# Moving the first expert's weight loads behind the last load of v, in a fused attention and mixture-of-experts kernel

## The chip, the cores and the metric

The kernel runs on one core of one Trainium2 chip, in one launch. The metric is the device time of the launch in microseconds (us). The core has TensorE (PE, with its weight loads as PEld), VectorE (DVE), ScalarE (ACT), GpSimd (POOL) and SyncE (SP); each runs its own instructions in the order in which they were written. In this kernel SP does nothing but issue DMA transfers, and a transfer that has to wait for something holds up those behind it on SP.

## The reference

Three stages follow one another. Attention is chunked: chunks of 32 queries see 16 keys to the left, 8 to the right and 8 memory keys. Its output, 3072 tokens of 512 features, goes through a top-2 mixture of 8 experts and then through a product with a maximum over three matrices.

```python
for c in range(nc):                                   # chunks of 32 queries
    scores = scale * np.matmul(q_c, k_full.transpose(0, 1, 3, 2))
    a = np.exp(scores - np.max(scores, axis=-1, keepdims=True))
    out[:, :, c_start:c_end] = np.matmul(a / (np.sum(a, axis=-1, keepdims=True) + 1e-09), v_full)
...
noisy_logits = x @ w_gate + np.log1p(np.exp(x @ w_noise)) * noise
top2 = np.argpartition(-noisy_logits, 2, axis=1)[:, :2]        # two experts per token
h = np.maximum(x[mask] @ w1[e], 0.0)
out[mask] += top2_w[mask, k, None] * (h @ w2[e])
...
h = np.maximum(np.maximum(x @ w1, x @ w2), x @ w3)
return h @ w_out
```

## The kernel before

**Attention** is a software pipeline over 24 tiles of 128 tokens. `step(t)` writes, in this order: the load of k and q for tile t + 6 (for even t), the scores of tile t + 2, the product with v of tile t (`pv`), the maximum and shift of tile t + 2 on DVE (`shift`), its exponential on ACT (`expo`), the copies of k for tile t + 4 on ACT (`windows`), the transposes of P for tile t + 1 (`ptrans`, into `pt` through ACT), the transposes of the output of tile t - 1 (`xtrans`, into `xt` through ACT), the gate of tile t - 2, some steps of the routing (`pump`, mostly small DVE work), the normalisation of tile t (`norm`: x on DVE, then SP stores x in DRAM as `xd`), and last the load of v for tile t + 3 (`load_v`, two transfers on SP into one of three buffers). Scores lie in one bank of PSUM, sc. The last scores are written in step 21, since step t computes those of tile t + 2.

**Weights** of the experts come as 512 KB parts. `wload` has SP load the next part into one of three staging tiles `st`. `wsplit` turns a part into a high and a low half: ACT copies st into the rounded high half (line 216, CAST), then DVE subtracts it from st to get the low half (line 213), and then the next `wload` follows. Matmuls take three passes (high by high, high by low, low by high). Parts 0 to 3 are w1 of expert 0, parts 4 to 7 its w2, parts 8 to 11 w1 of expert 1.

**Around the change.** Before, three loads are issued after step 15 (WL = 15), and from step 19 on one split follows each step (WS = 19), each with the next load behind it: parts 0 to 4 are split when attention ends, and parts 0 to 7 have their load issued. Unit 0, the first 384 tokens of expert 0, starts at once: eight column blocks f of the first product (12 matmuls each: four tiles of w1 by three passes), which alternate between two PSUM banks, sc and pp. Each is followed by a relu on ACT and the low half of h on DVE, and by one of the remaining splits: seven of them, spread over the eight blocks (none after f = 3). Between unit 0's matmuls `tail` puts what is left of attention (`xtrans` of the last two tiles, their gates) and of the routing (the one-hot tables oh and rc on DVE, their matmuls into tabp on PE). xT, the transposed tokens of unit 0, are gathered from xd and turned in the last steps (`unit_turn`: transposes into the bank xp, a CAST on ACT at line 193 and a subtraction on DVE at line 194).

Tokens for the units after the first can be gathered only when the routing of all tiles is done.

Of the kernel before, what the change touches and what calls it, by code (L numbers as in the profile page):

```python
# [23 lines left out]
NT = N // 128  # L24
# [7 lines left out]
PU = [1, 3, 5]  # L32
HOLD = 1
OHN = 4
WL = 15
WS = 19
NV = 3
RG = [6, 4, 3, 5, 3, 3]
G0 = 2
# [11 lines left out]
def tile_kernel(ctx, tc, qT, kT, mkT, vw, wgn, noise, w1, w2, m2w, out):  # L51
    nc = tc.nc
    PE, ACT, DVE, POOL, SP = nc.tensor, nc.scalar, nc.vector, nc.gpsimd, nc.sync
# [41 lines left out]
    def spin(o, n, joined=False):  # L95

        for i in range(n):
            if n == 10:
                mm(o, ones_r[:, 0:128], ones_r[:, 0:512], start=not joined or i == 0, stop=not joined or i == n - 1)
            else:  # L100
                mm(o, ones, warm, start=(i == 0), stop=(i == n - 1))
# [72 lines left out]
    def wtile(i):  # L174
        return slots[i % WB]

    def wload():
        n = wnext[0]
        if n == len(wparts):
            return  # L180
        wnext[0] += 1
        if isinstance(wparts[n], int):
            src = wsrc[wparts[n]] if wparts[n] < W0 else m2f[wparts[n] - W0]
            st = wst[n] = stage.tile([128, 1024], F32, name="st")
            o = st.rearrange("p (i d) -> p i d", i=2) if len(src.shape) == 3 else st
            SP.dma_start(o, src)
        else:
            _, j, h = wparts[n]
            st = wst[n] = stage.tile([128, 1024], I32, name="st")
            SP.dma_start(st, m2i[j, :, 1024 * h:1024 * h + 1024])  # L190
# [4 lines left out]

    formed = []

    def wsplit(eng=None):
        for task in wtasks()[1:]:
            task(eng)  # L200

    def wtasks():

        n = wnext[1]
        if n == len(wparts):
            return [n]
        wnext[1] += 1
        st = wst.pop(n)
        if isinstance(wparts[n], int):
            w = wtile(wparts[n])  # L210

            def low(eng):
                (eng or POOL).tensor_tensor(w[:, 1, :], st, w[:, 0, :].bitcast(F32), op=ALU.subtract)  # L213
                wload()

            return [n, lambda eng: ACT.copy(w[:, 0, :], st), low]  # L216
        _, j, h = wparts[n]
        return [n] + narrow(st.rearrange("p (n t) -> p n t", t=2), j, h)
# [77 lines left out]
    def unit_turn(u, j):  # L296
        if u < len(units) and j < len(fetched[u]):
            g, n = fetched[u][j]
            turn(g, n, xTs[u], 128 * j, None if u else 0)
# [14 lines left out]
    def load(t):  # L314
        b, i = divmod(t, TB)
        if i == 0:
            m_t[b] = ld.tile([128, HP, 8], F32, name="mk", bufs=2)
            SP.dma_start(m_t[b], mkT[b])
        if i % 2 == 0:
            eng = SP if t < 6 else ACT  # L320
            k_t[t] = ld.tile([128, HP, 280], F32, name="k")
            q_t[t] = ld.tile([128, 2, HP, 128], F32, name="q")
            for j in range(2) if t == 0 else [slice(0, 2)]:
                ks = slice(0, 280) if t else slice(152 * j, 152 + 128 * j)
                eng.dma_start(k_t[t][:, :, ks], kT[b, i // 2, :, :, ks])
                eng.dma_start(q_t[t][:, j], qT[b, i // 2, :, j])
            k_t[t + 1], q_t[t + 1] = k_t[t], q_t[t]
# [223 lines left out]
    def pump(n, tensor=True):  # L551

        for r in routes:
            r[1] -= 1
        moved = 1
        while n > 0 and moved:
            moved = 0
            for r in routes[:]:
                if n and r[1] <= 0 and (r[2] not in ("rank", "count", "table") or tensor) and (
                        r[2] != "rank" or r[3] == ranked[0]) and (r[2] != "table" or r is routes[0]):  # L560
                    r[2] = next(r[0], "end")
                    n, moved = n - 1, 1
                    if r[2] == "end":
                        routes.remove(r)
                    elif r[2]:
                        r[1] = hold[0]
# [19 lines left out]
    def turns_of_first():  # L586
        if 0 in fetched:
            turned[0] += 1
            if turned[0] > UH:
                unit_turn(0, turned[1])  # L590
                turned[1] += 1

    def do(f, u, *pr):
        if 0 <= u < NT:
            f(u, *pr)

    def pairs(f, t):
        for pr in range(HP):
            do(f, t, pr)

    def step(t):
        if t + 6 < NT and t % 2 == 0 and t >= 0:
            load(t + 6)
        pairs(scores, t + 2)
        if t <= 0:
            spin(idle, 10 if t < 0 else 6, t == -1)
        pairs(pv, t)
        do(shift, t + 2)
        do(expo, t + 2)
        do(windows, t + 4)  # L610
        pairs(ptrans, t + 1)
        if t < NT - 2:
            pairs(xtrans, t - 1)
            pairs(gate, t - 2)
        turns_of_first()
        pump(PU[1], False)
        do(norm, t)
        if t == NT - 2:
            pairs(gate, t - 2)
            pairs(xtrans, t - 1)  # L620
        if t >= 0:
            do(load_v, t + NV)
        if t < NT - 2:
            pump(PU[2], False)
        else:
            pump(PL)
# [13 lines left out]
    for t in range(-2, NT):  # L640
        step(t)
        if t == WL:
            for _ in range(3):
                wload()
        if t >= WS:
            wsplit(DVE)
        turns_of_first()
    while 0 not in fetched:
        pump(1000)
    while turned[1] < 4:  # L650
        unit_turn(0, turned[1])
        turned[1] += 1
    passing.close()


# [123 lines left out]
    def task_of(part, now, i):  # L779
        if i == 0:  # L780
            now += wtasks()
            assert wparts[now.pop(0)] == part
        now[i](DVE)

    def unit(u):
# [3 lines left out]
        if u == 0:  # L789
            side = spread([partial(wsplit, DVE)] * (len(plan[0]) + 8 - wnext[1]), 8) + [[] for _ in range(8, steps)]  # L790
        else:
            side = [[] for _ in range(steps)]
            for part, *at in plan[u]:
                now = []
                for i, t in enumerate(at):
                    side[t].append(partial(task_of, part, now, i))
# [77 lines left out]
    def second(xT, dst, step=lambda s: None, middle=lambda s: None, along=[]):  # L874

        h = [big.tile([128, 2, 512], F32R, name=f"h{i}") for i in range(6)]
        for f in range(3):
            ms = big.tile([128, 2, 512], F32, name=f"h{6 + f % 2}")
            for w in range(3):
                l = quads.pop(3 * f + w)  # L880
                for r in range(2):
                    step(6 * f + 2 * w + r)
                    p = psum("p")
                    for k in range(4):
                        if k == 2:
                            middle(6 * f + 2 * w + r)
                        three(p, [l[:, (k // 2) ^ (3 * r), k % 2, c, :] for c in range(2)],
                              parts(xT, k, slice(0, 512)), k == 0, k == 3)
                    m = ms[:, r, :]
                    if w == 0:  # L890
                        ACT.copy(m, p)
                    else:
                        DVE.tensor_tensor(m, m, p, op=ALU.max)
                    if w == 2:
                        split(m, h[2 * f + r][:, 0, :], h[2 * f + r][:, 1, :], DVE)
        step(18)
        side = spread(along, 24)
        side[4].insert(0, partial(middle, 19))
# [110 lines left out]
    def block(b):  # L1009
        t0, nt = blocks[b]  # L1010

        def step(s):
            if nt == 8:
                for k, task in ((8, block_turn), (0, block_fetch), (6, block_mix)):
                    if s >= k and (s - k) % 7 == 0:
                        task(b + 1, (s - k) // 7)
                return
            if s % 2 == 0 and s >= 4:
                block_mix(b + 1, s // 2 - 2)
            if b == 0 and s in (1, 3, 5):  # L1020
                quad_load((6, 7, 8)[s // 2])
            if b == 0 and s in (2, 5, 8):
                wsplit(DVE)
            if b == 0 and s == 6:
                ring_load()
            if b == 0 and s == 18:
                for _ in range(3):
                    ring_load()
# [125 lines left out]
```

## Time and profile before

| | |
|---|---|
| median of 3 runs | 1154.63 us (1151.62 to 1158.38) |
| the profiled execution's own time | 1149.49 us |
| its span, first to last instruction | 1147.7 us |
| mean granted TensorE clock | 0.995 of full |
| PE busy | 1106.3 us, 96% of the span |
| DVE, ACT, POOL busy | 55%, 34%, 19% of the span |

The profiled execution was 5.1 us shorter than the median of the runs, and 1.8 us of its time lie outside its span. PE is busy nearly everywhere after the first 165 us, so what a change before that point does to the end is read from when PE gets through the work of that stretch.

### The profile page before, as it was taken

The page shows a single profiled execution, that of the slowest core. Times are in us where ns is not written, and L with a number is a line of the kernel's source. Part 1 is how long each engine was busy: PE and PEld are TensorE (multiplying, and loading weights), DVE is VectorE, ACT ScalarE, POOL GpSimd, SP SyncE. Part 2 cuts the span into 40 slices and gives each one's busy share as a digit, 9 for nine tenths or more (in the row PEclk, how much of TensorE's full clock was granted, in tenths as well). Part 3 has the DMA queues.
Part 4 walks back from the last instruction along what each step waited for, and adds up shares of the span by engine and source line. Part 5 has one row for each costly group of instructions (what it writes and reads, how often), then busy time and mean ns, then how long its engine had stood idle before and what let it go on. Part 6 is the DMA issues. An engine that isn't in the chain of part 4 may idle for free. (4 is left out here: it accounts for less than half of the span.)

```text
span 1147.7 us, 17323 instructions
## 1 busy us (share of the span) xinstructions
PE 1106.3 (96%) x6803; PEld 927.2 (81%) x6804; DVE 632.7 (55%) x1258; ACT 391.6 (34%) x680; POOL 215.9 (19%) x237
## 2 busy tenths in 40 slices
PE   7987899999999999999999999999999999999997
PEld 5876778889888888888888887888877878887886
DVE  4586873373474645755646645334765586655221
ACT  5777432232422423424324233222411252113110
POOL 3001010100001001100110020243365525533000
PEclk9999899999999999999999999999999999999999
DMA  8998551261473554755834765375577635668301
GB/s 246 301 291 275 178 167 56 96 214 61 145 247 101 159 172 128 221 149 173 248 97 156 233 192 198 125 230 178 147 220 219 213 120 160 199 182 276 128 1 40
DMA packets 113689, 199.06 MB, mean 173 GB/s; under 512 B 8576, under 2 KB 46592, under 8 KB 113600
## 3 DMA queue, kind: packets, MB, share of 16 engines
q1 hardware_dynamic: 76736, 109.86, 30.4%
q0 software_dynamic: 34272, 78.13, 22.6%
q10 hardware_dynamic: 2592, 9.88, 2.8%
q8 instruction: 56, 0.92, 0.3%
q14 instruction: 33, 0.27, 0.1%
HBM read 151.18 MB, written 46.66 MB: 172 GB/s over the span
## 5 line engine op out<-in xcount | busy, mean ns | idle before, releaser
L93 PE MATMUL sc<-xT,w 128*128 128x512 f32 (+3 forms) x912 | 193.6, 359 | 5.1 <-DVE h L811 3.8
L93 PE MATMUL pp<-xT,w 128*128 128x512 f32 (+3 forms) x912 | 190.5, 356 | 0.0
L93 PEld LDWEIGHTS sc<-xT,w 128*128 128x128 f32 x912 | 157.3, 188 | 29.1 <-ACT h L807 3.1
L93 PEld LDWEIGHTS pp<-xT,w 128*128 128x128 f32 x912 | 157.4, 188 | 19.5 <-DVE h L811 0.2
L264 POOL DMA_INDIRECT g<-xd,tok x56 | 55.1, 984 | 531.3 <-PE idle L271 242.4
L93 PE MATMUL po<-w,h 128*128 128x512 f32 x548 | 135.0, 395 | 0.0
L93 PE MATMUL misc<-w,h 128*128 128x512 f32 x522 | 127.8, 394 | 0.0
L93 PE MATMUL tabp<-w,h 128*128 128x512 f32 x498 | 121.5, 394 | 0.0
L93 PEld LDWEIGHTS po<-w,h 128*128 128x128 f32 x548 | 101.0, 188 | 20.5
L93 PEld LDWEIGHTS misc<-w,h 128*128 128x128 f32 x522 | 96.5, 188 | 19.8
L93 PEld LDWEIGHTS tabp<-w,h 128*128 128x128 f32 x498 | 92.2, 188 | 18.9
L811 DVE SCALAR_TENSOR_TENSOR h<-sc,h 128x256 fp32r<-128x256 f32 (+2 forms) x96 | 39.9, 443 | 91.0 <-ACT h L807 91.0
L213 DVE TENSOR_TENSOR w<-st,w 128x1024 fp32r<-128x1024 f32 x67 | 81.0, 1217 | 11.2 <-ACT w L216 11.0
L811 DVE SCALAR_TENSOR_TENSOR h<-pp,h 128x256 fp32r<-128x256 f32 (+2 forms) x96 | 39.9, 443 | 71.6 <-ACT h L807 71.6
L216 ACT CAST w<-st 128x1024 fp32r<-128x1024 f32 x67 | 70.1, 1046 | 4.4 <-DMA st<-in_w 4.0
L807 ACT ACTIVATE h<-sc 128x512 fp32r<-128x512 f32 (+3 forms) x64 | 33.1, 517 | 111.4 <-PE sc L93 108.7
L264 POOL DMA_INDIRECT g<-ys,rows x48 | 50.6, 1053 | 101.3 <-DMA ys<-y 61.9
L807 ACT ACTIVATE h<-pp 128x512 fp32r<-128x512 f32 (+3 forms) x64 | 33.1, 517 | 80.3 <-PE pp L93 80.2
L93 PE MATMUL po<-v,pt 128*32 128x130 f32 x768 | 30.1, 294 | 17.7 <-ACT pt L383 8.9
L251 ACT CAST top<-val 128x1024 fp32r<-128x1024 f32 x18 | 18.9, 1049 | 80.2 <-DVE val L246 68.3
L194 DVE TENSOR_TENSOR xT<-xp,xT 128x512 fp32r<-128x512 f32 (+1 forms) x35 | 23.3, 666 | 37.8 <-ACT xT L193 37.8
L93 PEld LDWEIGHTS po<-v,pt 128*32 128x32 f32 x768 | 22.3, 115 | 24.2 <-ACT pt L383 12.6
(197 smaller groups left out, 1564.4 us busy)
## 6 DMA issues: line engine op xcount, KB each, us to landing
st<-in_w SPq DMA_DIRECT2D x64, 512.0 KB
w<-m2s POOLq DMA_DIRECT2D x27, 1024.0 KB
st<-in_m2w SPq DMA_DIRECT2D x24, 512.0 KB
ys<-y SPq DMA_DIRECT2D x48, 256.0 KB
m2s<-top SPq DMA_DIRECT2D x18, 512.0 KB
m2s<-val SPq DMA_DIRECT2D x18, 512.0 KB
xT<-m2s POOLq DMA_DIRECT2D x9, 1024.0 KB
w<-m2s POOLq DMA_DIRECT2D x9, 768.0 KB
```

The lines of the kernel that those rows point to most:

```text
L93: PE.matmul(o, l, r, start=start, stop=stop)
L194: (eng or POOL).tensor_tensor(lo, src, hi.bitcast(F32), op=ALU.subtract)
L213: (eng or POOL).tensor_tensor(w[:, 1, :], st, w[:, 0, :].bitcast(F32), op=ALU.subtract)
L216: return [n, lambda eng: ACT.copy(w[:, 0, :], st), low]
L251: ACT.copy(hi[0], full)
L264: POOL.indirect_dma_start(out=g[0:n], out_offset=None, in_=src, in_offset=bass.IndirectOffsetOnAxis(ap=idx, axis=0))
L807: ACT.activation(h[:, 0, 0:n], p[:, 0:n], AF.Relu)
L811: DVE.scalar_tensor_tensor(o[:, c], p[:, c], 0.0, h[:, 0, c].bitcast(F32), op0=ALU.max, op1=ALU.subtract)
```

## The change

The three first loads are issued after step 20, which is the step with the last load of v (WL = 20). Splits are written inside step 21, 22 and 23, right behind the place of the exponential (WS = 21): one in each of the first two, two in the last, so that four parts instead of five are split when attention ends. Only the first of these four is followed by a load (part 3); the other three loads, parts 4 to 6, are issued together after the last step. Unit 0 now has eight splits in its first product, one behind each block.

```diff
-WL = 15
-WS = 19
+WL = 20
+WS = 21
...
-    def wsplit(eng=None):
-        for task in wtasks()[1:]:
+    def wsplit(eng=None, more=True):
+        for task in wtasks(more)[1:]:
             task(eng)
...
                 (eng or POOL).tensor_tensor(w[:, 1, :], st, w[:, 0, :].bitcast(F32), op=ALU.subtract)
-                wload()
+                if more:
+                    wload()
...
         do(expo, t + 2)
+        if t >= WS:
+            for _ in range(1 + (t == NT - 1)):
+                wsplit(DVE, t == WS)
         do(windows, t + 4)
...
-        if t >= WS:
-            wsplit(DVE)
         turns_of_first()
     while 0 not in fetched:
         pump(1000)
     while turned[1] < 4:
         unit_turn(0, turned[1])
         turned[1] += 1
+    for _ in range(3):
+        wload()
     passing.close()
```

In the rows that follow, the numbers after a tile's name tell its allocations apart; w0 to w8 are the parts, P the shifted scores, L375/L376 their exponential. First SP, from the store of x of tile 20 to the first parts that unit 0 splits. Before:

```order
L401 DMA xd_57<-x_1846 128x512
L334 DMA v2_136<-in_vw 56x1040 x2
L186 DMA st_1858<-in_w2 128x2x512
L401 DMA xd_57<-x_1921 128x512
L186 DMA st_1932<-in_w2 128x2x512
L401 DMA xd_57<-x_1971 128x512
L186 DMA st_1999<-in_w2 128x2x512
L401 DMA xd_57<-x_2032 128x512
L186 DMA st_2052<-in_w2 128x2x512
```

And after the change:

```order
L402 DMA xd_57<-x_1836 128x512
L335 DMA v2_136<-in_vw 56x1040 x2
L186 DMA st_1846<-in_w1 128x1024
L186 DMA st_1848<-in_w1 128x1024
L186 DMA st_1850<-in_w1 128x1024
L186 DMA st_1893<-in_w1 128x1024
L402 DMA xd_57<-x_1917 128x512
L402 DMA xd_57<-x_1965 128x512
L402 DMA xd_57<-x_2026 128x512
L186 DMA st_2044<-in_w2 128x2x512
```

The first expert's w1 now stands behind the last v, and its w2 behind the last store of x (tile 23). Second, ACT from the exponential of tile 22 to the first turn of xT (L193). Before:

```order
L216 CAST w0_122<-st_1460 128x1024
L375 ACTIVATE P_1817<-P_1817 128x512
L383 COPY pt_1824<-pp_93 128x512
L409 COPY xt_1830<-xp_95 128x512
L216 CAST w1_123<-st_1462 128x1024
L375 ACTIVATE P_1896<-P_1896 128x512
L383 COPY pt_1903<-pp_93 128x512
L409 COPY xt_1909<-xp_95 128x512
L216 CAST w2_124<-st_1464 128x1024
L193 CAST xT0_130<-xp_95 128x4x128
```

And after the change:

```order
L376 ACTIVATE P_1807<-P_1807 128x512
L384 COPY pt_1814<-pp_93 128x512
L410 COPY xt_1820<-xp_95 128x512
L376 ACTIVATE P_1888<-P_1888 128x512
L217 CAST w0_122<-st_1846 128x1024
L384 COPY pt_1899<-pp_93 128x512
L410 COPY xt_1905<-xp_95 128x512
L193 CAST xT0_130<-xp_95 128x4x128
L217 CAST w1_123<-st_1848 128x1024
```

The two casts ahead of the exponentials of tiles 22 and 23 are gone, and the first cast stands between the exponential of tile 23 and pt of tile 22. Third, DVE between the last turn of xT (L194) and x of tile 23. Before:

```order
L424 TENSOR_TENSOR csum0_118<-csum1_119,add_1994 128x8
L213 TENSOR_TENSOR w3_125<-st_1780,w3_125 128x1024
L194 TENSOR_TENSOR xT0_130<-xp_95,xT0_130 128x4x128
L424 TENSOR_TENSOR pr_2023<-E1_109,idle_94 128x80
L485 TENSOR_REDUCE rank_115<-pr_2023 128x2x5
L396 TENSOR_SCALAR rs_2029<-po_96 128x8
L397 RECIPROCAL rs_2029<-rs_2029 128x8
L399 TENSOR_TENSOR x_2032<-po_96,rs_2029 128x512
```

And after the change:

```order
L425 TENSOR_TENSOR csum0_118<-csum1_119,add_1988 128x8
L194 TENSOR_TENSOR xT0_130<-xp_95,xT0_130 128x4x128
L213 TENSOR_TENSOR w2_124<-st_1850,w2_124 128x1024
L213 TENSOR_TENSOR w3_125<-st_1893,w3_125 128x1024
L425 TENSOR_TENSOR pr_2017<-E1_109,idle_94 128x80
L486 TENSOR_REDUCE rank_115<-pr_2017 128x2x5
L397 TENSOR_SCALAR rs_2023<-po_96 128x8
L398 RECIPROCAL rs_2023<-rs_2023 128x8
L400 TENSOR_TENSOR x_2026<-po_96,rs_2023 128x512
```

One split ahead of the turn became two behind it, ahead of the routing's pr and rank and of x. In unit 0 every block's split moves by one part: behind f = 0 stands part 4 where part 5 stood, and behind f = 3, where none stood, part 7.

## Rows read from the trace of the kernel before

**Rows 1.** The page: busy tenths of PE in 40 slices of the span.

```profile
PE   7987899999999999999999999999999999999997
```

**Rows 2.** Windows: each engine's busy us (instructions), granted clock, DMA share, GB/s.

```profile
120.00:140.00 20.00, 16.79 (x172) 14.79 (x163) 16.12 (x49) 10.44 (x19) 0.00 (x0) 0.83 0.50 157
140.00:160.00 20.00, 18.58 (x129) 17.25 (x128) 18.16 (x57) 9.72 (x17) 0.00 (x0) 1.00 0.52 161
180.00:200.00 20.00, 20.00 (x99) 18.24 (x98) 6.61 (x19) 4.91 (x9) 0.00 (x0) 1.00 0.01 3
```

**Rows 3.** Timeline of PE: start, us, instructions, idle before and its releaser.

```profile
89.84 1.08 PE L93 MATMUL sc<-kw,q 128*32 128x128 f32 x32
...
104.53 1.08 PE L93 MATMUL sc<-kw,q 128*32 128x128 f32 x32
107.88 1.96 PE L93 MATMUL po<-v,pt 128*32 128x130 f32 x32 [2.27 <-ACT P L375]
...
112.47 1.08 PE L93 MATMUL sc<-kw,q 128*32 128x128 f32 x32
...
117.80 1.08 PE L93 MATMUL sc<-kw,q 128*32 128x128 f32 x32
...
134.02 1.33 PE L93 MATMUL sc<-xT,w 128*128 128x384 f32 x3
```

**Rows 4.** Timeline of SP: when transfers were issued.

```profile
93.09 1.62 SPq L186 DMA_DIRECT2D st<-in_w  x3
...
99.16 1.72 SPq L334 DMA_DIRECT2D v<-in_vw  x2
...
119.26 0.37 SPq L401 DMA_DIRECT2D xd<-x  x1
...
126.55 0.38 SPq L186 DMA_DIRECT2D st<-in_w  x1
```

**Rows 5.** DMA view, 80 to 160 us: issues and KB (1024 bytes) of each.

```profile
st<-in_w SPq DMA_DIRECT2D x13, 512.0 KB
xd<-x SPq DMA_DIRECT2D x11, 256.0 KB
v<-in_vw SPq DMA_DIRECT2D x10, 227.5 KB
```

**Rows 6.** Windows around the loads and the slow clock, columns as in rows 2.

```profile
93.00:107.00 14.00, 10.65 (x211) 9.19 (x209) 10.84 (x33) 10.41 (x15) 0.00 (x0) 1.00 1.03 319
108.00:111.00 3.00, 3.00 (x43) 2.61 (x43) 0.66 (x4) 1.59 (x2) 0.01 (x1) 0.50 0.42 132
120.20:125.10 4.90, 2.78 (x34) 2.35 (x28) 4.61 (x21) 2.37 (x4) 0.00 (x0) 0.99 0.89 252
128.00:130.00 2.00, 1.48 (x12) 1.38 (x10) 0.67 (x2) 1.37 (x3) 0.00 (x0) 0.90 0.69 255
```

**Rows 7.** Timeline of ACT and DVE around steps 19 to 21.

```profile
108.68 0.94 ACT L346 COPY kw<-k 64x896 f32<-64x896 f32 x1
...
114.67 1.23 DVE L213 TENSOR_TENSOR w<-st,w 128x1024 fp32r<-128x1024 f32 x1 [2.94 <-ACT w L216]
...
119.82 1.23 DVE L213 TENSOR_TENSOR w<-st,w 128x1024 fp32r<-128x1024 f32 x1 [0.31 <-ACT w L216]
...
122.73 0.63 ACT L375 ACTIVATE P<-P 128x512 f32<-128x512 f32 x1 [2.94 <-DVE P L372]
123.27 0.57 ACT L383 COPY pt<-pp 128x512 f32<-128x512 f32 x1
```

**Rows 8.** Timeline of DVE, ACT and PE in unit 0.

```profile
134.93 0.69 DVE L399 TENSOR_TENSOR x<-po,rs 128x512 f32<-128x512 f32 x1
...
138.41 1.04 ACT L216 CAST w<-st 128x1024 fp32r<-128x1024 f32 x1
139.35 0.59 ACT L409 COPY xt<-xp 128x512 f32<-128x512 f32 x1
...
140.30 0.37 PE L93 MATMUL tabp<-rc,oh 128*128 128x56 f16 x8
...
141.11 0.51 PE L93 MATMUL misc<-wg_sb,xt 128*128 128x16 f32 x4
...
151.71 0.32 PE L93 MATMUL tabp<-rc,oh 128*128 128x56 f16 x6 [0.67 <-DVE rc L424]
```

More of the change, by code (lines that the diff above doesn't have):

```diff
@@ L196, in tile_kernel, with wtasks @@
     formed = []
-    def wsplit(eng=None):
-        for task in wtasks()[1:]:
+    def wsplit(eng=None, more=True):
+        for task in wtasks(more)[1:]:
             task(eng)
-    def wtasks():
+    def wtasks(more=True):
         n = wnext[1]
```

## The prediction

> **What bounds the kernel now.** I began with the page's line of PE in slices: PE is at nine tenths or more from the eighth slice on and has its gaps in the first six, some 170 us [rows 1]. The windows by 20 us say which stretch is loose: PE is busy 16.8 of 20 us from 120 to 140, at a mean clock of 0.83, 18.6 from 140 to 160, and all of 180 to 200 [rows 2]. So the change can only win or lose where it is made, between the loads at 93 us and some 165 us, and what it does to PE there it does to the end. In that stretch DVE is the second engine to look at: 16.1 and 18.2 of 20 us busy [rows 2].
>
> The timeline of PE shows the end of attention step by step, by the starts of the scores [rows 3]. Steps 16 to 18 took (104.53 - 89.84) / 3 = 4.90 us each, step 19 took 7.94. In it PE stood 2.27 us ahead of the product with v of tile 19, and that product then took 1.96 us where the scores, of the same count, take 1.08. The page names ACT's exponential as what PE waited for, but v of tile 19 is the likelier one: its load was issued at 99.16, behind the three weight loads of 93.09 [rows 4], while the DMA engines were busy without a break (share 1.03 at 319 GB/s from 93 to 107) [rows 6]. Three loads are 3 x 524 = 1573 thousand bytes [rows 5], 4.9 us at that rate. From 108 to 111 the granted clock was 0.50 [rows 6], that is 1.2 instead of 2.4 GHz, after PE had stood; 3 us at half rate cost 1.5 us.
>
> **The change part by part.** I follow one number, the lead: how much earlier than before the same instruction comes.
>
> *Step 19, won.* Without weight loads in front, v of tile 19 lands some 4.9 us earlier, which is more than the 2.27 us it was late. The lead at step 20 lies between 7.94 - 4.90 = 3.0 and 2.27 + 1.5 = 3.8 us. ACT's last copy of k ends at 109.6 [rows 7] and pt of tile 20 comes behind it, so not all of this is free; I take 3.5.
>
> *Steps 20 and 21, won.* DVE's two splits at 114.67 and 119.82 (1.23 us each) stood ahead of the shifts of tiles 22 and 23 [rows 7]. The scores of 22 were done at 112.47 + 1.08 = 113.55 and the first split at 115.9, so the shift came 2.3 us late; the second split ended at 121.05, and DVE had other work up to 119.5, so 1.5 late. Both together are worth between 2.5 (the splits alone) and 3.8; I take 3.2, since the routing's exponentials on ACT then come next. The exponential of tile 23 moves from 122.73 [rows 7] by 6.7 to 116.0 and ends at 116.65. The store of x of tile 20 stands ahead of the second split, so it wins less: 5.2, from 119.26 [rows 4] to 114.1.
>
> *The first cast, lost.* Behind that exponential ACT now meets the cast of part 0, and pt of tile 22 is queued behind it, which PE's product of tile 22 waits for. When does part 0 land? Before, the same three things stood in a row on SP: xd, the two halves of the last v, one weight load; 262 + 466 + 524 = 1252 thousand bytes [rows 5]. From 120.20 to 125.10 the engines moved 4.9 x 252 = 1235 [rows 6], so the load landed at about 125.1, 5.8 us after xd was issued. The load is now issued some 0.5 us sooner behind v: I take 5.3, that is 119.4. The nearest bound below is a load by itself: issued at 126.55 [rows 4], moved from 128 to 130 (510 thousand bytes) [rows 6], 3.45 us, which from 115.4 gives 118.8. The bound above is that the second and third load take a share meanwhile; the next rival prices it. ACT stands from 116.65 to 119.4, casts for 1.04, and pt of tile 22 comes at 120.45 instead of 123.27 [rows 7]: the lead falls to 2.8. PE stands longer than before at this place, so I leave it the stretch at half rate that it had there. Parts 1 to 3 land 1.6 to 2 us after one another and are not waited for. Part 3's load waits on SP for the split of part 0, with the stores of x of tiles 21 to 23 queued behind it; x of tile 21 comes after that split on DVE anyway, so this costs nothing.
>
> The Trainium skill (DMA: Bandwidth & Descriptors, section Queues, rings and completion order) says that each DMA engine consumes the descriptors of a ring in order; by that rule part 0 is not slowed by parts 1 and 2, the landing at 119.4 stands and with it the 0.7 us of the sum, and without it B's 4.2 would be due. No row here shows one of three queued loads landing.
>
> *Unit 0's start.* From there the chain (turns, product of tile 23) is the same; the first matmul moves from 134.02 [rows 3] to 131.2.
>
> *Two splits in a row, lost on DVE.* Behind the last turn DVE now has the low halves of parts 2 and 3, ACT their two casts, where before one split stood ahead of the turn. That is one split more (1.23) and about 1.0 us of waiting for the first cast ahead of pr, rank and x of tile 23: x, at 134.93 [rows 8], has a lead of only 0.6 us and starts at 134.3.
>
> *The cast of part 4, lost on ACT.* Its load stands behind xd of tile 23 on SP, so it is issued at about 135.5 and lands, by the 3.45 us of the lone load, at 138.9. ACT meets the cast behind the relu of f = 0, which comes 2.8 us earlier than before, and so it waits some 3 us. Queued behind it is xt of tile 23, which ends at 140.6 (before: 139.35 + 0.59 = 139.94 [rows 8]). PE needs it for the gate of tile 23, at 141.11 [rows 8]: with xt at 140.6 the lead is 0.5. The tables ahead of it (140.30) don't decide: rc comes 0.6 us earlier by DVE's lead and 1.2 by the split of part 4 that no longer stands in front.
>
> *The split behind f = 3, lost.* DVE gets 1.22 us more just where PE already waits 0.67 us for its rc at 151.71 [rows 8], in a window where DVE is 91% busy [rows 2]. Between 0 (if DVE's idle 1.8 us of that window take it) and 1.22; PE's wait says that there is no slack, and I take 1.2. Ahead of it 0.5 was left, so PE is 0.7 us late, and stays so.
>
> Sum: + 3.5 + 3.2 - 3.9 - 2.3 - 1.2 = -0.7, so 0.7 us longer. The profiled execution's own 1149.5 would be 1150.2; on the median of the runs, 1154.63, that is **1155.3 us**.
>
> **The rivals.** *A: the lead holds.* The parts land as lone loads do, DVE takes the extra splits into its idle time (3.9 and 1.8 us from 120 to 160 [rows 2]), and the gates wait for nothing; the 2.8 us at unit 0's first matmul reach the end: 1151.8. For it: PE, not DVE, is nearly full there. Against it: the rc wait, and that xd of tile 23 must be stored before part 4 is loaded. It decides if part 4 lands before about 136.7.
>
> *B: slower, the three loads land together.* Then ACT waits for 262 + 466 + 3 x 524 = 2300 thousand bytes instead of 1252, at 300 GB/s 3.5 us more, and everything behind pt of tile 22 is that much later: 0.7 + 3.5 = 4.2, 1158.8. It begins to decide when part 0 lands after 120.7, and from 118.7 on there is nothing left to win. For some of it speaks that 252 GB/s from 120.20 to 125.10 is less than the 319 of the fuller stretch [rows 6], so a load can be slow; against it, that the load of before landed about when its own bytes and those ahead of it were through. The rule of the Trainium skill on ring order above speaks against it too. A second stretch at half rate in unit 0, after the waits for rc and xt, would cost 1.5 us and comes on top.
>
> *C: the change doesn't do what it says.* If v of tile 19 is late through k, q and v alone, step 19 stays at 7.94, and the rest gives 0.7 + 3.5 = 4.2 us: 1158.8 as well. The bytes speak against it: without the loads the busy stretch would be 4.9 us shorter.
>
> **How the numbers follow.** My forecast, with its own bounds (part 0 between 118.8 and 120.7, the last split between 0 and 1.2), is 1153.5 to 1156.6: 0.56. A 0.23, B 0.15, C 0.06. A range of 1151.0 to 1158.8 takes in the middle of each, and about 2 in 10 of the chance lie outside. A measurement of this kernel can tell about 0.5% from no change, here 5.8 us. No case gives that much by itself: a faster result needs A with the half clock gone too (0.08), a slower one B or C with a second stretch at half rate (0.07). Within 0.5%: 0.85.
>
> **What would show it.** In the profile after: step 19 at about 4.5 to 5 us and no half clock near 108; the cast of part 0 with a wait of 2 to 3 us for the DMA behind the exponential of tile 23; unit 0's first matmul near 131; x of tile 23 near where it was; a wait of ACT for part 4's load of about 3 us; PE's wait for rc in the fifth routing group grown from 0.67 to nearly 2 us, and the last table matmuls within 1 us of before. I am wrong if the casts don't wait, or if routing ends as much earlier as unit 0 starts.

## The result and the profile after

The changed kernel is slower: 1161.82 us (median of 9 runs) against 1151.8 us (9 runs of before), a ratio of 1.0094 [1.0078, 1.011]. The prediction was 1155.3 us with a range up to 1158.8, so it was wrong. It counted from 1154.63, the median of the first three runs of before; in its own terms it expected 0.7 us more than before, and 10.0 us came.

The profiled execution took 1160.44 us with a span of 1158.6. It is already 1.14 us behind the one of before at the scores of tile 18 (90.98 us against 89.84 in [rows 3]), ahead of everything that the change touches; I take that off below. The timeline of PE, columns as in [rows 3]:

```profile
90.98 1.08 PE L93 MATMUL sc<-kw,q 128*32 128x128 f32 x32
...
100.56 1.08 PE L93 MATMUL sc<-kw,q 128*32 128x128 f32 x32
...
104.28 1.08 PE L93 MATMUL sc<-kw,q 128*32 128x128 f32 x32
106.98 1.09 PE L93 MATMUL po<-v,pt 128*32 128x130 f32 x32 [1.62 <-ACT pt L384]
...
109.98 1.08 PE L93 MATMUL sc<-kw,q 128*32 128x128 f32 x32
...
126.27 1.12 PE L272 MATMUL xp<-ident,g 128*128 128x128 f32 x4 [6.23 <-ACT xt L410]
128.00 1.96 PE L93 MATMUL po<-v,pt 128*32 128x130 f32 x32 [0.62 <-DVE x L400]
...
137.08 1.33 PE L93 MATMUL sc<-xT,w 128*128 128x384 f32 x3
...
147.80 0.62 PE L93 MATMUL misc<-wg_sb,xt 128*128 128x16 f32 x4 [2.75 <-ACT xt L410]
...
150.92 2.27 PE L93 MATMUL sc<-xT,w 128*128 128x384 f32 x6
...
162.43 0.32 PE L93 MATMUL tabp<-rc,oh 128*128 128x56 f16 x6 [1.64 <-DVE rc L425]
...
173.97 0.32 PE L93 MATMUL tabp<-rc,oh 128*128 128x56 f16 x6 [1.10 <-DVE rc L425]
```

Two things are to be seen. The start is won, though not quite where it was forecast: step 19 takes 109.98 - 104.28 = 5.70 us where it took 7.94 (forecast: 4.5 to 5), with PE still waiting 1.62 us for pt. The product with v runs at full speed, and there is no slow stretch near 108 us. Then PE stands twice, 6.23 us ahead of 126.27 and 2.75 us ahead of 147.80, each time for a copy of xt on ACT. In [rows 8] the gate of tile 23 stood at 141.11, without a wait.

The last tables come at 173.97 us. Before, the same group stood 11.5 us behind the 151.71 of [rows 8], as here behind 162.43:

```profile
163.20 0.32 PE L93 MATMUL tabp<-rc,oh 128*128 128x56 f16 x6 [1.10 <-DVE rc L424]
```

What follows is alike: 1158.6 - 173.97 = 984.6 us here, 1147.7 - 163.20 = 984.5 before. So the whole loss lies ahead of the last tables. ACT's timeline shows what xt waited for:

```profile
118.98 0.63 ACT L376 ACTIVATE P<-P 128x512 f32<-128x512 f32 x1 [2.35 <-DVE P L373]
124.20 1.04 ACT L217 CAST w<-st 128x1024 fp32r<-128x1024 f32 x1 [4.59 <-DMA st<-in_w]
125.15 0.58 ACT L384 COPY pt<-pp 128x512 f32<-128x512 f32 x1
125.63 0.59 ACT L410 COPY xt<-xp 128x512 f32<-128x512 f32 x1
...
146.22 1.04 ACT L217 CAST w<-st 128x1024 fp32r<-128x1024 f32 x1 [4.50 <-DMA st<-in_w]
147.17 0.58 ACT L410 COPY xt<-xp 128x512 f32<-128x512 f32 x1
```

Both casts wait for their load some 4.5 us, with pt and xt queued behind them. The timeline of SP says when the loads were issued; a row joins issues that follow each other:

```profile
117.05 0.37 SPq L402 DMA_DIRECT2D xd<-x  x1
...
118.35 8.51 SPq L186 DMA_DIRECT2D st<-in_w  x4
127.97 13.06 SPq L402 DMA_DIRECT2D xd<-x  x3
141.13 7.78 SPq L186 DMA_DIRECT2D st<-in_w  x4
```

Part 0 arrives for ACT 7.15 us after xd was issued (124.20 - 117.05), and part 4 5.1 us after its own issue at 141.13; the prediction gave them 5.3 and 3.45. The windows of the same execution, columns as in [rows 2]:

```profile
120.00:140.00 20.00, 12.09 (x117) 10.26 (x117) 10.92 (x33) 9.13 (x16) 0.00 (x0) 0.66 0.42 142
140.00:160.00 20.00, 16.83 (x100) 15.81 (x99) 13.52 (x41) 7.70 (x15) 0.00 (x0) 0.83 0.51 168
...
121.80:126.20 4.40, 0.00 (x0) 0.00 (x0) 0.92 (x1) 2.00 (x3) 0.00 (x0) 0.50 0.74 294
126.20:131.40 5.20, 4.51 (x43) 3.61 (x44) 4.31 (x19) 1.84 (x4) 0.00 (x0) 0.50 0.49 151
...
149.00:154.00 5.00, 5.00 (x25) 4.39 (x24) 2.81 (x8) 1.52 (x3) 0.00 (x0) 0.50 0.51 147
```

Against [rows 2] PE does 4.7 us less work from 120 to 140 and 1.8 less from 140 to 160. In the first stand and behind each of the two the granted clock is 0.50 (1.2 of 2.4 GHz) for a while. The lead, 1.14 us taken off, as predicted and as measured:

| place | predicted lead, us | measured lead, us |
|---|---|---|
| scores at 112.47 of [rows 3] | 3.5 | 3.6 |
| exponential of tile 23 | 6.7 | 4.9 |
| pt of tile 22 | 2.8 | -0.7 |
| unit 0's first matmul | 2.8 | -1.9 |
| gate of tile 23 | 0.5 | -5.5 |
| tables of the fifth group | -0.7 | -9.6 |

### The profile page after: what moved, and what is told of

Its sections match the earlier page's. It is cut to its first block, busy times and chain, and to the rows that moved or that the text cites. A ratio compares the mean times of both kernels' runs of the same rounds, so it can differ in the third digit from the quotient of the medians.

```text
span 1158.6 us, 17319 instructions
## 1 busy us (share of the span) xinstructions
PE 1109.7 (96%) x6803; PEld 930.6 (80%) x6804; DVE 632.9 (55%) x1258; ACT 392.2 (34%) x680; POOL 216.3 (19%) x237
## 5 line engine op out<-in xcount | busy, mean ns | idle before, releaser
L213 DVE TENSOR_TENSOR w<-st,w 128x1024 fp32r<-128x1024 f32 x67 | 81.0, 1218 | 16.3 <-ACT w L217 16.1
L194 DVE TENSOR_TENSOR xT<-xp,xT 128x512 fp32r<-128x512 f32 (+1 forms) x35 | 23.3, 666 | 39.0 <-ACT xT L193 38.9
L193 ACT CAST h<-h 128x128 fp32r<-128x128 f32 (+1 forms) x60 | 18.2, 363 | 66.8 <-DVE h L897 51.7
```

The costliest lines, as they stand in the source:

```text
L193: ACT.copy(hi, src)
L194: (eng or POOL).tensor_tensor(lo, src, hi.bitcast(F32), op=ALU.subtract)
```

## The experiments

My theory was that the two waits for loads are the whole loss, and that the load arrives later than the bytes moved per us say. The rivals: the loads slow one another (the prediction's B), the new place of the splits costs by itself, or the half rate does. "Before" in the ratios is run on the same chip beside each.

| run | what it is | median, us | ratio to before |
|---|---|---|---|
| the change | both waits | 1161.82 | 1.0094 [1.0078, 1.011] |
| e1_loads_early | first loads behind step 15 | 1158.6 | 1.0061 [1.0041, 1.008] |
| e2_first_alone | part 0 loaded alone | 1161.8 | 1.0088 [1.0064, 1.0113] |
| e3_loads_follow | each split followed by its load | 1154.6 | 1.0030 [1.0012, 1.0048] |
| e4_wl17 | first loads behind step 17 | 1155.98 | 1.0049 [1.0028, 1.007] |
| e6_wl17_follow | both of these | 1151.02 | 0.9995 [0.9978, 1.0012] |
| e7_before_wl17 | before, first loads behind step 17 | 1148.09 | 0.9976 [0.9961, 0.999] |
| e8_split_end | e3, splits at the ends of the steps | 1154.9 | 1.0042 [1.0024, 1.0061] |
| e9_spin | the change, matmuls into the wait | 1158.63 | 1.0072 [1.005, 1.0094] |
| e10_gather | e6, gathers later | 1149.06 | 0.9987 [0.9972, 1.0002] |
| e11_ws20_wl17 | e6, splits from step 20 on | 1150.28 | 0.9998 [0.9981, 1.0016] |
| e12_before_wl17_gate | e7, gathers later | 1146.98 | 0.9971 [0.9954, 0.9989] |

### Loads early, and the first load alone

**e1_loads_early** is the change with `WL = 15` as before; the splits and the last three loads stay in their new places.

```
-WL = 20
+WL = 15
```

> The changed kernel, but its first three loads are issued after step 15, as before the change; splits and the loads of parts 4 to 6 stay where the change put them. Theory 1 (the loss is two waits of ACT for loads, 4.6 us at the cast of part 0 and 4.5 us at that of part 4, with what PE loses behind them): the first wait goes, the stand ahead of the product with v of tile 19 comes back (2.3 us and a stretch at half rate), the second wait stays near 4.5 us; some 5 to 7 us above the kernel before, 3 to 5 below the changed one. Rival (the place of the splits costs: ahead of pt, two in a row ahead of x of tile 23, one more behind f = 3): no better than the changed kernel, 10 us above before.

The first cast waits for nothing (122.24 us). The cast of part 4 still waits 4.20 us and the gate of tile 23 2.50. v is late again: PE waits 2.15 us for it, here in step 17. Steps 17 to 19 together take 18.1 us, as before the change, against 14.5 in the change. So against before, which stands there too, most of the loss is left without the first wait.

**e2_first_alone** loads part 0 alone behind the last v, and the next parts only behind later steps.

```
-                wsplit(DVE, t == WS)
+                wsplit(DVE, False)
...
-        if t == WL:
-            for _ in range(3):
-                wload()
+        for _ in range({20: 1, 21: 2, 22: 1}.get(t, 0)):
+            wload()
```

> The changed kernel, but only part 0 is loaded behind the last v; parts 1 and 2 are issued behind the store of x of tile 21, part 3 behind that of tile 22. If part 0 lands late because the loads of parts 1 and 2 share the DMA engines with it: ACT's wait at the cast of part 0 falls from 4.6 to 2 to 3 us and part 0 lands 5 to 5.5 us after the store of x of tile 20 is issued (7.15 in the changed kernel). If it is late because a load behind the last v takes that long anyway: the wait stays at 4 to 5 us. In total 0 to 3 us below the changed kernel by the first, within 1 us of it or slower by the second.

ACT still waits 4.29 us for part 0 (4.59 in the change), so the parts behind it slow it by 0.3 us at most, and rival B falls. By itself the load shows what the prediction left out. The windows by 1 us, the last column the GB/s (here also the thousand bytes moved in the window):

```profile
118.00:119.00 1.00, 0.80 (x32) 0.56 (x25) 0.91 (x6) 0.17 (x1) 0.00 (x0) 1.00 0.01 4
119.00:120.00 1.00, 1.00 (x31) 0.80 (x23) 0.97 (x4) 0.00 (x0) 0.00 (x0) 1.00 0.61 213
120.00:121.00 1.00, 1.00 (x13) 1.00 (x10) 0.48 (x1) 0.49 (x1) 0.00 (x0) 1.00 0.74 207
121.00:122.00 1.00, 0.57 (x6) 0.47 (x5) 0.00 (x0) 0.14 (x1) 0.00 (x0) 1.00 0.93 241
122.00:123.00 1.00, 0.00 (x0) 0.00 (x0) 0.00 (x0) 0.00 (x0) 0.00 (x0) 1.00 0.96 198
123.00:124.00 1.00, 0.00 (x0) 0.00 (x0) 0.00 (x0) 0.00 (x0) 0.00 (x0) 0.67 0.97 381
124.00:125.00 1.00, 0.00 (x0) 0.00 (x0) 0.00 (x0) 0.00 (x0) 0.00 (x0) 0.50 0.08 29
```

The end of it in windows of 0.2 us, and the cast:

```profile
124.80:125.00 0.20, 0.00 (x0) 0.00 (x0) 0.00 (x0) 0.00 (x0) 0.00 (x0) 0.50 0.05 20
125.00:125.20 0.20, 0.00 (x0) 0.00 (x0) 0.00 (x0) 0.00 (x0) 0.00 (x0) 0.50 0.00 0
```

```profile
125.43 1.04 ACT L217 CAST w<-st 128x1024 fp32r<-128x1024 f32 x1 [4.29 <-DMA st<-in_w]
```

From 118 to 124 us 4 + 213 + 207 + 241 + 198 + 381 = 1244 thousand bytes moved, nearly as many as xd, v and part 0 have (1252). Nothing is queued behind them. Yet the load is not over at 124: a share of 0.05 stays until 125.0, about what one of the core's 16 DMA engines makes (1/16 = 0.06), and then there is nothing. The load is complete only when its slowest engine is through, about 1 us behind the rest. The cast starts at 125.43, 0.4 us after the last bytes and 1.4 us after the point at which the sum of the bytes says that the load is there. The Trainium skill (DMA: Bandwidth & Descriptors, section Anatomy of one DMA — SWDGE (gpsimd) path) says that the semaphore update can't fire until the last byte is confirmed landed; the trace agrees, as the cast starts behind the last engine's bytes. The Trainium skill puts, in the same section, about 2.0 us of fixed cost on a transfer, most of it that confirmation, for GpSimd's path; this load went by SP, and its trace shows 0.4 us. Why one engine is behind the others is not shown.

### One wait at a time

**e3_loads_follow** issues a load behind each split, as before the change, and drops the three loads behind attention. Part 4 is then issued early, part 0 as in the change.

```
-                wsplit(DVE, t == WS)
+                wsplit(DVE)
...
-    for _ in range(3):
-        wload()
```

> The changed kernel, but each split is followed by its load, as before the change, so that parts 4 to 6 are loaded in steps 22 and 23 and not together behind the store of x of tile 23. Theory 1: the wait at the cast of part 4 (4.5 us), PE's wait for xt behind it (2.75 us) and the stretch at half rate near 150 us go, the wait at the cast of part 0 stays; 4 to 6 us below the changed kernel. Rival (place of the splits): within 1 us of the changed kernel.

It came 0.64% below the change, a little more than the 4 to 6 us expected. On ACT the first wait stays (4.23 us), the second is gone:

```profile
122.09 1.04 ACT L217 CAST w<-st 128x1024 fp32r<-128x1024 f32 x1 [4.23 <-DMA st<-in_w]
...
139.19 1.04 ACT L217 CAST w<-st 128x1024 fp32r<-128x1024 f32 x1
```

**e4_wl17** is the change with `WL = 17`, so that the first wait goes and the second stays.

> The changed kernel with nothing but the step of the first loads changed, 17 instead of 20: part 0 is there when its cast comes, while part 4's load still stands behind the last store of x. With it the four cases of the two waits are complete: neither (0.9995), the first alone (1.0030), both (1.0094). If the two waits add up, the second alone stands at 0.9995 + 0.0064 = 1.006, with the cast of part 4 waiting some 4 us and the gate of tile 23 some 2.5. If the first wait only makes the second worse (the half rate behind it, the late store), the second alone costs less, 1.002 to 1.004.

```profile
120.97 1.03 ACT L217 CAST w<-st 128x1024 fp32r<-128x1024 f32 x1
...
142.04 1.04 ACT L217 CAST w<-st 128x1024 fp32r<-128x1024 f32 x1 [5.61 <-DMA st<-in_w]
```

The gate of tile 23 waits 2.60 us, and the matmuls behind it run at half rate, 1.31 us for three. The 1.0049 lies between the two expectations.

**e6_wl17_follow** has both edits: `WL = 17`, and each split followed by its load.

> Both waits taken away at once: the changed places of the splits, but the first three loads are issued after step 17 (behind the v of tile 20, so that the v of tile 19 is ahead of them) and each split is followed by its load. Theory 1: no cast waits for a load, PE does not stand at tile 19; 0 to 4 us below the kernel before. Rival (place of the splits): 4 us or more above the kernel before.

No cast waits, and the loss is gone. The four cases fit together: over e6 the first wait costs 0.35%, the second 0.54%, both 0.99%. A plain sum would be 0.89%, and each ratio is known to about 0.2%, so whether the two make each other worse can't be told. It is shown, though, that with neither nothing of the loss is left that this measurement could tell (0.2%).

### What stands behind the waiting cast, and the clock

**e8_split_end** is e3 with the splits at the ends of the steps, so that pt of tile 22 and xt of tile 20 stand ahead of the first cast on ACT.

```
-        if t >= WS:
-            for _ in range(1 + (t == NT - 1)):
-                wsplit(DVE)
         do(windows, t + 4)
...
+        if t >= WS:
+            for _ in range(1 + (t == NT - 1)):
+                wsplit(DVE)
         turns_of_first()
```

> The loads as in the run with each split followed by its load (first load behind step 20), but the splits at the ends of steps 21 to 23, so that ACT meets the first cast behind pt of tile 22 and xt of tile 20 and no longer ahead of them. That run stood at 1.0030 [1.0012, 1.0048]. If its loss comes from pt of tile 22 queued behind the waiting cast, this run comes back to the kernel before: 0.999 to 1.001, and pt of tile 22 comes some 4 us earlier than there. If the loss comes from the late part itself (the casts and splits behind it late, whatever waits in front), it stays near 1.003.

pt goes ahead, and the time does not come back: 1.0042, no better than e3's 1.0030. ACT's timeline, and then PE's:

```profile
120.66 0.56 ACT L384 COPY pt<-pp 128x512 f32<-128x512 f32 x1
...
126.22 1.04 ACT L217 CAST w<-st 128x1024 fp32r<-128x1024 f32 x1 [4.51 <-DMA st<-in_w]
```

```profile
129.18 1.11 PE L272 MATMUL xp<-ident,g 128*128 128x128 f32 x4 [5.15 <-DVE xT L194]
```

The same lateness now goes through DVE: the split waits for the cast, the copy of unit 0's turn (xT) is queued behind the split, and PE waits for that. This profile was of the slowest of twelve runs, 1160.94 us, so only the order of its waits is read here.

**e9_spin** is the change with 48 matmuls of 250 columns whose result nothing reads, put where ACT waits for part 0.

```
+        if t == 21:
+            for i in range(48):
+                mm(po_b[:, 1, 262:512], ones, warm[:, 0:250], start=(i == 0), stop=(i == 47))
```

> The changed kernel with 48 matmuls of 250 columns added in step 21, into a stretch of PSUM that nothing reads, ahead of unit 0's turns: they keep TensorE at work while ACT waits for the first load. If the half rate of TensorE behind that wait costs something by itself, the granted clock stays at 1.00 through the wait, the product with v of tile 22 takes about 1.1 us instead of 1.96, and the run is 1.5 to 3 us faster than the changed kernel (ratio to before near 1.007). If the half rate lies beside DVE's work and costs nothing, the clock rises all the same but the time stays within 0.5 us of the changed kernel's 1.0094. If the added matmuls run longer than the wait, it is slower by what they overrun.

PE's timeline, then ACT's pt of tile 22, then a window:

```profile
117.09 5.28 PE L93 MATMUL po<-warm,ones 128*128 128x250 bf16 x48
...
125.21 1.09 PE L93 MATMUL po<-v,pt 128*32 128x130 f32 x32 [1.07 <-DVE x L400]
```

```profile
122.36 0.58 ACT L384 COPY pt<-pp 128x512 f32<-128x512 f32 x1
```

```profile
120.00:140.00 20.00, 15.17 (x174) 13.15 (x172) 15.25 (x52) 9.46 (x17) 0.00 (x0) 1.00 0.43 141
```

The clock stays up, the product with v takes 1.09 us and not 1.96. The median is 3.2 us below the change's, but the intervals of the two ratios overlap, and the wait for part 4 grew from 4.50 to 5.75 us: part of what was won is waited for there. What the clock alone is worth can't be told from the 3.2 us either. On this chip the maxima of tile 22 did not wait as they did in the profile of the change (see e10 below), and this profile is 2.4 us ahead of it at the exponential of tile 23, counted from the scores of tile 18; from there to unit 0's first matmul it gains another 2.5 us.

### The place of the splits

**e7_before_wl17** is the kernel before with `WL = 17`, and nothing else.

> The kernel before, with nothing changed but the step behind which the first three weight loads are issued: 17 instead of 15. The splits stay at the ends of the steps. The run with the same loads and the splits behind the exponentials stood at 0.9995 of the kernel before. If the place of the splits is worth nothing and only the loads' times decide, this run lies within 2 us of that one, some 1150 to 1152 us, with no cast waiting for a load. If the place of the splits matters (the two splits ahead of the shifts of tiles 22 and 23 were costed at 3.2 us in the prediction), this run is slower than that one by about 3 us, ratio near 1.002 to 1.003.

It came out faster than e6, on the side that neither expectation had: 0.9976 against 0.9995, though the two intervals overlap. In its timeline of DVE the split does hold the shift of tile 22, as the prediction said of before:

```profile
113.52 1.23 DVE L213 TENSOR_TENSOR w<-st,w 128x1024 fp32r<-128x1024 f32 x1 [3.54 <-ACT w L216]
114.66 0.68 DVE L369 TENSOR_REDUCE mx<-sc 128x8 f32<-128x512 f32 x1
```

The scores were done at 111.2 us, so the shift came 3.5 us late, and the scores of tile 23 waited 2.11 us for it on PE. Yet the run loses nothing at the end. Counted from the scores of tile 18, unit 0's first matmul comes after 41.1 us here and after 38.6 in e13 (e6's program, below), where no split stands ahead of the shifts and the maxima don't wait. At the tables of the fifth group the two are level, 58.5 and 58.4 us. So between these two profiles moving the splits wins some 2.5 us up to unit 0, and their new places give it back behind: PE's wait for rc alone is 1.78 us there for 0.64. They are single profiles, from two chips.

**e11_ws20_wl17** is e6 with `WS = 20`, one split more in attention and none behind f = 3.

> The run with loads behind step 17, each split followed by its load and the splits behind the exponentials (0.9995 of the kernel before), with the splits begun one step earlier: five in attention, so that in unit 0 no split stands behind f = 3 any more. The same loads with the splits at the ends of the steps, also five in attention, stood at 0.9976. If the split behind f = 3 is the difference between the two, TensorE's wait for rc in the fifth group falls from 1.79 us to about 0.65, and the run stands near 0.9985 to 0.9975. If it is where in the step the split stands, the run stays near 0.9995, with the smaller wait all the same. A run below 0.9976 would say that the place behind the exponential is worth something.

PE's wait for rc falls as expected, and the time stays where it was:

```profile
150.48 0.32 PE L93 MATMUL tabp<-rc,oh 128*128 128x56 f16 x6 [0.64 <-DVE rc L425]
```

The split behind f = 3 does cost PE 1.1 us at that place (1.79 in e6), but e11 shows no such gain in the time. (v of tile 18 was 1.39 us late in it, but steps 17 to 19 took 14.5 us all the same, as in e6.) Between 0.9998 and 0.9976 the difference of e11 and e7 is hardly more than the two measurements allow; what makes it, if it is real, stays open. One candidate is in the traces: with a split inside step 21, PE's product of tile 22 waits 0.6 to 1.1 us for x of tile 21 on DVE, in all ten such profiles, and in none of the four with the splits at the ends of the steps.

**e10_gather** is e6, and **e12_before_wl17_gate** is e7, each with a small copy on GpSimd of tile 22's maxima ahead of unit 0's gathers.

```
+        if pend and 0 not in fetched:
+            POOL.tensor_copy(tiny, mx.rearrange("p h a o -> p (h a o)"))
+            unit_fetch(0)
...
-            unit_fetch(0)
+            pend.append(0)
```

> The run with loads behind step 17 and each split followed by its load, with one small copy on GpSimd of tile 22's maxima put ahead of unit 0's three gathers, so that they start only when DVE has those maxima. In every run so far the maxima of tile 22 started 2.4 to 3.7 us late, while the scores were done, TensorE stood in short gaps and GpSimd was at work on the gathers. If the gathers hold DVE there, the maxima now start within 0.3 us of the scores' end, the exponential of tile 22 comes about 2 us earlier, and the wait moves behind them or goes: 0 to 2 us faster than the 0.9995 of the run without the copy. If something else holds DVE, the wait of 2.4 us or more stays where it is and the time is the same within 0.1 %.

> The kernel before with the first loads behind step 17 (0.9976), and one small copy on GpSimd of tile 22's maxima ahead of unit 0's gathers, so that these start behind the maxima. If the gathers at their old place cost DVE or TensorE time, this run is up to 2 us faster, 0.996 to 0.9976. If they cost nothing there, it is the same, or slower by what the gathers' later start costs the first turn, up to 3 us.

In the change the maxima of tile 22 stood 3.70 us idle with no releaser on the core, 2.5 us behind the end of the scores, and PE's product with v had gaps, while GpSimd issued the gathers (from 109.09 on). In e10 wait and gaps are gone. But they are gone too in three other runs on that chip with the gathers where they were, so e6 was run once more.

**e13_wl17_follow_again** is e6, unchanged, on another chip.

> The same kernel as the run with loads behind step 17 and each split followed by its load, for one look. In its first profile the maxima of tile 22 waited 3.70 us and TensorE's product with v had four gaps of 0.3 us while the gathers ran; four later profiles of other kernels, with the gathers at the same place, show neither. If the program decides, wait and gaps are here again. If something outside the program does, they are gone, and the copy ahead of the gathers cannot be held to have removed them.

The maxima of tile 22 on DVE, first in e6, then in e13:

```profile
114.48 0.69 DVE L370 TENSOR_REDUCE mx<-sc 128x8 f32<-128x512 f32 x1 [3.70 <-remote]
```

```profile
112.80 0.69 DVE L370 TENSOR_REDUCE mx<-sc 128x8 f32<-128x512 f32 x1 [1.37 <-PE sc L93]
```

The same program shows the wait on one chip and not on another. So the copy can't be held to have removed it, and neither e10 nor e12 differs from its partner by more than the measurement.

Two versions beat both kernels: before with its first loads behind step 17, 0.9976 [0.9961, 0.999], and the same with the gathers later, 0.9971 [0.9954, 0.9989], some 3 us each. There the loads are behind v of tile 20 and still in time for every cast.

## Why the prediction was wrong, point by point

**Step 19, won: the cause right, the size partly by luck.** The lead at step 20 is 3.6 us, and 3.5 was taken, but step 19 gave only 2.2 of it, less than the lower bound of 3.0: PE still stood 1.62 us there, for pt. The other 1.4 us came in step 18, which the prediction had counted as undisturbed; it took 3.7 us for the 5.1 from 99.42 to 104.53 before:

```profile
99.42 1.08 PE L93 MATMUL sc<-kw,q 128*32 128x128 f32 x32
```

That the weight loads are the cause holds for the three steps together: steps 17 to 19 took 18.1 us in before and in e1, the two with the loads behind step 15, and 14.1 to 16.1 us in the twelve other profiles. So rival C falls. That PE waited for v of tile 19 in step 19 is not shown.

**Steps 20 and 21, won: wrong in size.** The lead at the exponential of tile 23 is 4.9 us, not 6.7. I gave the whole lateness of the two shifts to the splits; without them the maxima of tile 22 were 2.5 us late all the same, for a reason that the trace does not name. In e9, on a chip without that wait, the exponential comes 25.6 us behind the scores of tile 18 instead of 28.0, so the 6.7 would then have been reached. Since xd of tile 20 goes with it, this alone costs the first wait nothing, but everything behind comes 1.8 us later.

**The first cast, lost: the mechanism right, the term too small.** 4.59 + 1.04 us instead of 2.75 + 1.04. The step that failed is "so the load landed at about 125.1": that was where the sum of the bytes had moved. No row of before shows an engine released by a load there. In e2 the slowest DMA engine was through about 1 us behind the rest, and the cast started 0.4 us behind that. The order on SP's queue was right: the parts behind don't slow part 0 by more than 0.3 us.

**Unit 0's start: not the same chain.** It loses 1.2 us more. The step that failed is "x of tile 21 comes after that split on DVE anyway, so this costs nothing": it was said of the store of x, and left out that PE needs that x too. Before, x of tile 21 stood ahead of the split of its step; in the change it stands behind the split of part 0, which waits for the late cast. PE's product of tile 22 writes where that x is read, so it waits for x. DVE and PE before, then DVE in the change:

```profile
123.45 0.69 DVE L399 TENSOR_TENSOR x<-po,rs 128x512 f32<-128x512 f32 x1
```

```profile
124.96 1.96 PE L93 MATMUL po<-v,pt 128*32 128x130 f32 x32
```

```profile
125.28 1.23 DVE L213 TENSOR_TENSOR w<-st,w 128x1024 fp32r<-128x1024 f32 x1 [6.33 <-ACT w L217]
...
127.26 0.69 DVE L400 TENSOR_TENSOR x<-po,rs 128x512 f32<-128x512 f32 x1
```

The product starts 1.69 us behind pt of tile 22 before (124.96 - 123.27) and 2.85 us behind it in the change (128.00 - 125.15). It is not the half rate: in e9, at full rate, it is 2.85 us as well (125.21 - 122.36). From the product to unit 0's first matmul it takes 9.1 us in both, with the product of tile 22 and that of tile 23 at half rate in both (1.96 us).

**The cast of part 4, lost: right in mechanism, too small twice over.** The load was issued where I had said, behind xd of tile 23, but that came 5.6 us later (4.5 with the 1.14 taken off), and it took 5.1 us from its issue instead of 3.45. The errors of the terms ahead come back here, since the store of x stands at the end of the same chain, and what follows the bulk of the bytes is left out a second time. e4 shows that this wait alone costs 0.54%; that it costs more than the first (0.35%) is within the measurement.

**The half rate in unit 0: named, not summed.** I gave it 1.5 us, in a rival. Between the gate of tile 23 and the tables of the fifth group the lead falls by 4.0 us: PE's wait for rc takes 1.0 of them (1.64 for 0.67; 1.2 predicted), the other 3 are matmuls at half rate, such as six in 2.27 us for 1.31.

**Two splits in a row, and the split behind f = 3: right.** From unit 0's first matmul to x of tile 23 the lead falls by 2.0 us (2.2 predicted), and the wait for rc was as predicted, nearly 1.7 us. That this wait decides the end is not shown, since e11 without it is no faster than e6. With no load late, moving the splits is worth, on balance, nothing that I could tell from zero, or a little in favour of the ends of the steps.

So the sum went wrong by 8.9 us: 1.8 at the exponential, 1.8 at the first wait, 1.2 at unit 0's start, 1.3 at the second wait, 2.8 behind it.

## What to carry to other kernels

In this kernel a wait for a load ended when its slowest DMA engine was through and the waiting engine had been released, 1.4 us behind the point that the bytes moved per us gave. Take the arrival of a load from a row in which an engine does wait for one, and if there is none, widen the range by it. A cast that waits in order holds all that is queued behind it on its engine, and here changing the order only handed the lateness to the next engine (e8): move the load's issue. When a split moves on an engine, look at each later instruction there that others wait for (x of tile 21). Where PE stood for several us here, it ran at half rate behind (1.2 of 2.4 GHz), and where that stretch was not also there before the change, it belongs into the sum.

## What the runs showed of the hardware

The maxima of tile 22 waited 3.6 to 3.7 us, with no releaser on the core, in the profile of the change and in all five from two of the chips, and in none of those from two others that could show it, for the same program too (e6 and e13). Where they waited, PE's product with v had gaps of 0.3 us. What it is stays open. e13's profiled run was 1.9 us shorter than e6's (1147.73 against 1149.64), but single runs differ by more than that.

A load of 512 KB with nothing queued behind it (e2) had all but about one of its 16 DMA engines through shortly after 124.0 us; the last bytes moved until 125.0, and the waiting cast started at 125.43.
